# Splitting a half one step earlier, asking for an input first, and sending four outputs by another queue

## The chip, the cores and the metric

The kernel runs on one core of one Trainium2 chip. TensorE (PE in the rows) does the matmuls, VectorE (DVE) and ScalarE (ACT) the elementwise work, GpSimd (POOL) and SyncE (SP) mostly ask for transfers. Each engine takes its instructions strictly in the order in which they were written, so an instruction that waits holds up everything behind it on that engine. The metric is device time in microseconds (us). Smaller is better.

## The reference, cut to what matters

```python
def reference(...):
    x = attn(x)                          # a Fourier layer: (2, 3008, 256) -> 6016 tokens x 256
    h = x @ w_in                         # first layer, 2048 wide
    x = (h * clip(h + 3, 0, 6) / 6) @ w_out
    g = x @ w_gate                       # second layer, 1536 wide: the change lies here
    val = x @ w_val
    return (silu(g) * val) @ w_out2      # float32 throughout
```

## The kernel before

The kernel runs in three parts: the Fourier layer, the first layer, and the second layer (from 617 us on). The change lies in the second layer.

The 6016 tokens are cut into six pairs of halves (five pairs of 2 x 512 tokens, one of 2 x 448). A step works one pair against one block of 128 of the 1536 hidden columns, so a pair takes 12 steps and the layer has 72, counted q = 0 to 71. In a step the gate and value products of both halves are made by seven block products instead of eight (a scheme of sums and differences). Each float32 product is three matmuls on parts: a high part, which ScalarE casts, and a low part, the difference that VectorE takes (`low`, line 138). One product is three rows at lines 948, 949 and 950. In the order of the step on TensorE they are P (1), Tb (7), Q (2), P (6), Tb (4), P (5), and P (3), the last of which stands in the next step's code.

Each step follows one chain. `seed` copies P into Q (line 1316); ScalarE copies Tb (`c7`) and P (`cu`) into a ring `cc` before further products are added to those banks; `first_sum` adds `cu` to Tb (line 1321), silu follows (line 1322); `second_sum` adds `c7` to P (line 1327), silu follows (line 1308); the first half's result is h0 * Q (line 1254), the second half's h1 * P, once P (3) has been added. Both halves are then split into high and low (`parted`, lines 1292 and 138) and multiplied by the output weights into four accumulators (`share`, whose matmuls stand in `mm3`, lines 133 to 135; the third of them reads the low part).

Pair 0 (q = 0 to 11) and nearly all of the last pair (q = 61 to 71) run as `plain`, with four output products for each step: 33 matmuls in all. There the results of step q - 1 are split in the code of step q. The steps of pairs 1 to 4 run as `quad`; they take fewer output products, form sums of results of neighbouring steps (`units`, added on VectorE at line 1247 or by an adding transfer on POOL's queue at line 1250), and work on what remains in the next pair. The first quad, q = 12, still closes pair 0: it makes the last output products and sends four outputs of pair 0 (`outward`, `send_out`, line 1180).

Two side works run along. `operands` prepares the next pair's input: a load into `raw` (1 MB, one buffer, line 840), then eleven steps of one cast on ScalarE (line 806, in seven of them) and one subtraction on VectorE (lines 799 and 138). `todo.send()` does one of these at the end of each step. `out_sums` and `out_parts` prepare, in pair 0, the sums of the output weights for the middle pairs: in even steps four small subtractions on VectorE and one copy on ScalarE (lines 1222 to 1226), in odd steps two casts on ScalarE, two subtractions on VectorE and two transfers on POOL's queue (lines 1238 to 1243). Weights for a step come on SP's queue (`fetch`, line 868), asked for about three steps ahead into one of four slots.

Nothing schedules the work: the order on each engine is the order of the code.

Of the kernel before, what the change touches and what calls it, by code (L numbers as in the profile page):

```python
# [82 lines left out]
def fourier_moe_kernel(ctx: ExitStack, tc: tile.TileContext, x, lin, bias, w1, w2, fwd1, inv2, fwd2,  # L83
                       inv1, out):
    nc = tc.nc
# [179 lines left out]
    p = psf[0]([128, 512], "p0")  # L265
# [697 lines left out]
    todo = Todo()  # L963
# [136 lines left out]
    ring2 = {}  # L1100
# [73 lines left out]
        nc.tensor.matmul(o, wh, xh, start=False, stop=False, skip_group_check=True)  # L1174
        nc.tensor.matmul(o, wh, xl, start=False, stop=True, skip_group_check=True)

    def send_out(p, e, t, c, send=nc.sync):
        n = halves[p]
        at = pairs[p][0] + t * n
        send.dma_start(out[e * 128 : e * 128 + 128, at : at + n], c[:, :n])  # L1180
# [75 lines left out]
            nc.vector.scalar_tensor_tensor(out=o, in0=x, scalar=-1.0, in1=y, op0=ALU.mult, op1=ALU.mult)  # L1256

    def upper(before):
        p, k, odd, P, h, product, n = before
        product(P, 3)  # L1260
        times2(U(p, ("T3", "T2")[odd], k), h[:, :n], P[:, :n], 1 if odd else -1)

# [27 lines left out]
    def parted(x, n):  # L1290
        hi, lo = (take(c)[:, :n] for c in ("hi", "lo"))
        nc.scalar.copy(hi, x[:, :n])  # L1292
        low(lo, x[:, :n], hi)
        return hi, lo
# [20 lines left out]
    def seed(q, P, Q, n):  # L1315
        nc.scalar.copy(Q[:, :n], P[:, :n])  # L1316
        state.pop("silu", lambda: None)()
# [12 lines left out]
    def quad(q, before):  # L1330
        p, f = quads2[q]
        k, odd = divmod(f, 2)
        n = halves[p]
        old, i = p - 1, f
        waits, first = old > 0, q == NF
        a = (p, k - 1) if k else (p - 1, NK - 1)
        P, T = bank_p(F0 + q), one_bank(spot[0] + 3, [128, BLK], "Tb")
        if p == 1 and odd and f < NF - 1:
            Q = one_bank(spot[0], [128, BLK], "Q")
        else:  # L1340
            Q = bank_q([128, BLK], "Q")
        product = multiply(B[len(pairs) + p], F0 + q, n)
        product(P, 1, start=True)
        if waits:
            later(old, i, 0)
        else:
            product(T, 7, start=True)
        seed(q, P, Q, n)
        if first:
            x0 = parted(state["own"], n)  # L1350
            x1 = parted(upper_plain(before), n)
        else:
            upper(before)
        if waits:
            later(old, i, 1)
        if odd:
            x1 = halve(p, k, "T1")
            add_up(p, k, "T1", "T3")
            if a[0] > 0:
                add_up(*a, "T2", "T1")  # L1360
                add_apart(*a, "T4", "T2")
        elif a[0] > 0:
            x2, x3 = halve(*a, "T4"), halve(*a, "T2")
            add_up(*a, "T3", "T2")
        if waits and i % 3 == 2:
            phase(old, i // 3)
        if waits:
            product(T, 7, start=True)
        c7 = ring2["c"]()[:, :n]
        nc.scalar.copy(c7, T[:, :n])  # L1370
        if first:
            share(q, 0, 0, x0)
            outward(0, 0, 0)
        product(Q, 2)
        product(P, 6)
        if waits:
            ask(old + (i + 2) // NF, (i + 2) % NF)
        elif f == NF - 1:
            ask(1, 0)
            ask(1, 1)  # L1380
        if old + (i + 1) // NF > 0:
            part2(old + (i + 1) // NF, (i + 1) % NF)
        cu = ring2["c"]()[:, :n]
        nc.scalar.copy(cu, P[:, :n])
        if odd:
            live(p, 1, k, slot[F0 + q - 1][:, 14:16], x1)
            gone(q - 1)
            if f == NF - 1:
                then = begin(p)
        elif first:  # L1390
            share(q, 0, 1, x0)
            outward(0, 0, 1)
            share(q, 1, 0, x1)
        else:
            live(a[0], 2, a[1], slot[F0 + q - 1][:, 14:16], x2)
            if not k:
                corner(a[0])
        product(T, 4)
        h0 = first_sum(T, cu, n)
        if first:  # L1400
            outward(0, 1, 0)
            share(q, 1, 1, x1)
            gone(q - 1)
        elif not odd:
            live(a[0], 3, a[1], slot[F0 + q - 1][:, 16:18], x3)
            gone(q - 1)
            if not k:
                third(a[0])
        product(P, 5)
        h1 = second_sum(P, c7, n)  # L1410
        if first:
            outward(0, 1, 1)
            home.append(spots["double"])
        if q == len(quads2) - NF:
            own()
        times2(take("own")[:, :n] if p == len(pairs) - 1 else U(p, ("T1", "T4")[odd], k), h0, Q[:, :n],
               -1 if odd and p < len(pairs) - 1 else 1)
        state["own"] = spots["own"][-1]
        todo.send()
        silu(q, h1)  # L1420
        if f == NF - 1:
            then()
        return p, k, odd, P, h1, product, n

    def own():
        d = spots["double"] = home.pop()
        spots["own"] = [d[:, 0], d[:, 1]]

    def upper_plain(before):
        _, _, _, P, h, product, n = before  # L1430
        product(P, 3)
        s1 = take("own")
        times2(s1[:, :n], h[:, :n], P[:, :n], 1)
        return s1

    def plain(q, before):

        p, f = quads2[q] if q < len(quads2) else (None, None)
        pb = len(pairs) - 1 if q in LAST else 0
        old, i = pb - 1 if p else -1, f  # L1440
        n = halves[pb]
        early = old > 0 and f == 1
        if early:
            later(old, i, 0)
            later(old, i, 1)
        if before:
            s1 = upper_plain(before)
        if old > 0 and not early:
            later(old, i, 0)
            later(old, i, 1)  # L1450
        if before:
            x0 = parted(spots["own"][0], n)
        if p is None:
            x1 = parted(s1, n)
            for t, x in enumerate((x0, x1)):
                for e in range(2):
                    share(q, t, e, x)
                    if t and e:
                        a = acc.pop((t, e))
                        for o, c, copy, send in ((take("short"), slice(0, n // 2), nc.vector.tensor_copy, nc.sync),  # L1460
                                                 (take("h"), slice(n // 2, n), nc.scalar.copy, nc.scalar)):
                            copy(o[:, c], a[:, c])
                            at = pairs[pb][0] + n
                            send.dma_start(out[e * 128 : e * 128 + 128, at + c.start : at + c.stop], o[:, c])
                    else:
                        outward(pb, t, e)
            return None
        k, odd = divmod(f, 2)
        if early:
            add_up(old, NK - 1, "T2", "T1")  # L1470
            add_apart(old, NK - 1, "T4", "T2")
        T, Q = one_bank(spot[0] + 3, [128, BLK], "Tb"), bank_q([128, BLK], "Q")
        P = bank_p(F0 + (len(quads2) - NF if pb else q))
        product = multiply(B[len(pairs) + p], F0 + q, n)
        product(P, 1, start=True)
        if q == 0:
            fetch(F0 + 2)
            fetch(F0 + 3)
            nc.tensor.matmul(Q, slot[F0][:, 0], B[len(pairs)][1][:, 0], start=True, stop=True)
            end = end_of()  # L1480
            drain(2)
        seed(q, P, Q, n)
        if before:
            x1 = parted(s1, n)
        if old > 0 and i % 3 == 2:
            phase(old, i // 3)
        product(T, 7, start=True)
        c7 = ring2["c"]()[:, :n]
        nc.scalar.copy(c7, T[:, :n])
        if q == 0:  # L1490
            end()
            drain(2)
        else:
            share(q, 0, 0, x0)
        product(Q, 2)
        product(P, 6)
        if old > 0 and i + 1 < NF:
            part2(old, i + 1)
        if old > 0 and i + 2 < NF:
            ask(old, i + 2)  # L1500
        cu = ring2["c"]()[:, :n]
        nc.scalar.copy(cu, P[:, :n])
        if q == 0:
            drain(2)
        else:
            share(q, 0, 1, x0)
        product(T, 4)
        h0 = first_sum(T, cu, n)
        if q == 0:
            drain(len(pending))  # L1510
            lay_out_rest()
            own()
        product(P, 5)
        h1 = second_sum(P, c7, n)
        if q:
            share(q, 1, 0, x1)
            share(q, 1, 1, x1)
            gone(q - 1)
        times2(take("own")[:, :n], h0, Q[:, :n], 1)
        state["own"] = spots["own"][-1]  # L1520
        todo.send()
        silu(q, h1)
        if not p:
            (out_parts if odd else out_sums)(k)
        return p, k, odd, P, h1, product, n

    lay_out()
    ask_out(0)
# [69 lines left out]
```

## Time and profile before

| what | us |
|---|---|
| median of 3 runs | 1140.84 (1140.32 to 1141.79) |
| profiled execution | 1139.65 |
| its span in the trace | 1137.9 |
| TensorE busy | 1111.9 (98%) |
| VectorE busy | 963.4 (85%) |
| ScalarE busy | 803.8 (71%) |
| chain of waits: TensorE, VectorE, ScalarE, DMA | 78%, 12%, 4%, 3% |

Matmuls are pipelined: one that reads 512 columns shows 0.38 us, but the next starts 0.22 us after it. So the busy share of TensorE says little, and what is lost is read from the distance of two starts. An idle time that the trace gives in square brackets names the instruction that ended it.

### The profile page before, as it was taken

The page shows a single profiled execution, that of the slowest core. Times are in us where ns is not written, and L with a number is a line of the kernel's source. Part 1 is how long each engine was busy: PE and PEld are TensorE (multiplying, and loading weights), DVE is VectorE, ACT ScalarE, POOL GpSimd, SP SyncE. Part 2 cuts the span into 40 slices and gives each one's busy share as a digit, 9 for nine tenths or more (in the row PEclk, how much of TensorE's full clock was granted, in tenths as well). Part 3 has the DMA queues.
Part 4 walks back from the last instruction along what each step waited for, and adds up shares of the span by engine and source line. Part 5 has one row for each costly group of instructions (what it writes and reads, how often), then busy time and mean ns, then how long its engine had stood idle before and what let it go on. Part 6 is the DMA issues. An engine that isn't in the chain of part 4 may idle for free.

```text
span 1137.9 us, 19968 instructions
## 1 busy us (share of the span) xinstructions
PE 1111.9 (98%) x7397; PEld 973.0 (86%) x7397; DVE 963.4 (85%) x1703; ACT 803.8 (71%) x1491; POOL 72.7 (6%) x105
## 2 busy tenths in 40 slices
PE   8999999999999999999999999899999999999998
PEld 7989888888888888888999777687888888888997
DVE  6878887999999999999987676598999999998665
ACT  4767676788787887887777565567667777776555
POOL 3000016200000000000000000000000000000000
PEclk9999999999999999999999999899999999999999
DMA  7756335874474572753745554677877877878551
GB/s 286 292 183 226 121 109 190 269 234 167 148 241 152 167 254 99 234 214 106 257 145 185 217 199 176 217 231 232 259 231 227 261 248 231 263 240 249 195 199 74
DMA packets 82201, 234.18 MB, mean 206 GB/s; under 512 B 8180, under 2 KB 31892, under 8 KB 70648
## 3 DMA queue, kind: packets, MB, share of 16 engines
q1 hardware_dynamic: 75472, 216.20, 55.9%
q0 software_dynamic: 6336, 16.52, 5.4%
q8 instruction: 58, 0.95, 0.3%
q14 instruction: 39, 0.32, 0.1%
q10 hardware_dynamic: 296, 0.20, 0.1%
HBM read 180.98 MB, written 45.61 MB: 199 GB/s over the span
## 4 chain that ended last, share of the span: by engine, by line
PE 78%; DVE 12%; ACT 4%; DMA 3%; issue 2%; POOL 0%; DVEq 0%; ACTq 0%; SPq 0%; POOLq 0%
PE acc L135 8%; PE acc L133 8%; PE acc L134 8%; PE P L948 7%; PE P L950 6%; PE P L949 6%; PE Tb L948 3%; PE Tb L950 3%; PE Tb L949 3%; DMA raw<-Xd 2%; PE p L462 2%; PE p L368 2%; PE Q L948 2%; PE Q L949 2%; PE Q L950 2%
## 5 line engine op out<-in xcount | busy, mean ns | idle before, releaser
L618 ACT CAST gated<-r 128x512 fp32r<-128x512 f32 (+1 forms) x160 | 98.3, 614 | 64.4 <-DVE r L996 62.9
L138 DVE TENSOR_TENSOR gated<-r,gated 128x512 fp32r<-128x512 f32 (+1 forms) x160 | 107.9, 674 | 24.1 <-ACT gated L618 19.4
L133 PE MATMUL acc<-gated,w_o 128*128 128x512 f32 (+1 forms) x320 | 120.4, 376 | 0.0
L1322 ACT ACTIVATE hv<-hv 128x512 f32<-128x512 f32 (+1 forms) x72 | 44.8, 622 | 107.0 <-DVE hv L1321 107.0
L134 PE MATMUL acc<-gated,w_o 128*128 128x512 f32 (+1 forms) x320 | 119.6, 374 | 0.0
L135 PE MATMUL acc<-gated,w_o 128*128 128x512 f32 (+1 forms) x320 | 119.6, 374 | 0.0
L992 ACT ACTIVATE r<-hold,consts 128x512 f32<-128x512 f32 (+1 forms) x120 | 85.5, 712 | 14.2 <-DVE hold L1000 12.1
L948 PE MATMUL P<-xo,slot 128*128 128x512 f32 (+1 forms) x240 | 91.1, 380 | 2.4 <-DVE hold L1000 1.2
L950 PE MATMUL P<-xo,slot 128*128 128x512 f32 (+1 forms) x240 | 89.1, 371 | 0.0
L949 PE MATMUL P<-xo,slot 128*128 128x512 f32 (+1 forms) x240 | 89.1, 371 | 0.0
L996 DVE SCALAR_TENSOR_TENSOR r<-r,hold 128x512 f32<-128x512 f32 (+1 forms) x120 | 80.8, 674 | 2.5 <-ACT r L992 1.4
L1321 DVE TENSOR_TENSOR hv<-Tb,cc 128x512 f32<-128x512 f32 (+1 forms) x72 | 48.6, 675 | 33.9 <-PE Tb L950 33.9
L133 PEld LDWEIGHTS acc<-gated,w_o 128*128 128x128 f32 x320 | 60.5, 189 | 7.0
L135 PEld LDWEIGHTS acc<-gated,w_o 128*128 128x128 f32 x320 | 60.5, 189 | 6.9
L134 PEld LDWEIGHTS acc<-gated,w_o 128*128 128x128 f32 x320 | 60.5, 189 | 6.7
L133 PE MATMUL acc<-live,slot 128*128 128x512 f32 (+1 forms) x156 | 58.9, 378 | 0.8 <-ACT live L1292 0.8
L134 PE MATMUL acc<-live,slot 128*128 128x512 f32 (+1 forms) x156 | 58.4, 374 | 0.0
L948 PEld LDWEIGHTS P<-xo,slot 128*128 128x128 f32 x240 | 45.4, 189 | 13.5 <-DVE hold L1000 3.0
L1316 ACT COPY Q<-P 128x512 f32<-128x512 f32 (+1 forms) x72 | 40.8, 566 | 20.3 <-PE P L950 16.7
L1327 DVE TENSOR_TENSOR hv<-P,cc 128x512 f32<-128x512 f32 (+1 forms) x72 | 48.4, 672 | 6.1 <-PE P L950 6.1
L1153 ACT CAST parts<-units 128x1024 fp32r<-128x1024 f32 x48 | 50.5, 1052 | 0.0
L950 PEld LDWEIGHTS P<-xo,slot 128*128 128x128 f32 x240 | 45.5, 190 | 4.4
(251 smaller groups left out, 3332.9 us busy)
## 6 DMA issues: line engine op xcount, KB each, us to landing
slot<-Wd SPq DMA_DIRECT2D x48, 1024.0 KB
slot<-Sd SPq DMA_DIRECT2D x40, 896.0 KB
slot<-Wd SPq DMA_DIRECT2D x24, 1152.0 KB
st<-in_w SPq DMA_DIRECT2D x68, 256.0 KB
Wd<-slot SPq DMA_DIRECT2D x12, 1024.0 KB
chunk<-Vd SPq DMA_DIRECT2D x48, 256.0 KB
m<-in_fwd SPq DMA_DIRECT2D x12, 512.0 KB
Cd<-cs POOLq DMA_DIRECT2D x12, 512.0 KB, 5.1
```

Of the source, the lines that this page charges most:

```text
L133: nc.tensor.matmul(o, wl, xh, start=start, stop=False)
L134: nc.tensor.matmul(o, wh, xh, start=False, stop=False)
L135: nc.tensor.matmul(o, wh, xl, start=False, stop=stop)
L138: nc.vector.tensor_tensor(out=o, in0=full, in1=hi.bitcast(F32), op=ALU.subtract)
L618: nc.scalar.copy(hi[:, :n], g[:, :n])
L948: nc.tensor.matmul(o, wl, hi, start=start, stop=False, skip_group_check=not start)
L949: nc.tensor.matmul(o, wh, lo, start=False, stop=False, skip_group_check=not start)
L950: nc.tensor.matmul(o, wh, hi, start=False, stop=True, skip_group_check=not start)
L992: nc.scalar.activation(r[:, :n], x[:, :n], AF.Relu, bias=three)
L996: nc.vector.scalar_tensor_tensor(out=r[:, :n], in0=r[:, :n], scalar=6.0, in1=x[:, :n], op0=ALU.min, op1=ALU.mult)
L1153: nc.scalar.copy(hi, t[:, :, :n])
L1321: nc.vector.tensor_tensor(out=h, in0=T[:, :n], in1=cu, op=ALU.add)
```

## The change

It has five parts.

1. In pair 0 the first half's result is split at the end of its own step, in `plain`, and handed on with the other results; the next step only uses it.
2. In pair 0 `out_sums` and `out_parts` run in the next step's code, after the second half's split; the last of them falls into the first quad.
3. The first quad asks for the next pair's input (`todo.send()`) ahead of its other work, and not at its end.
4. The four outputs of pair 0 are asked for by POOL's queue, and not by SP's.
5. Two changes of order: in the steps of pair 1 ScalarE copies Tb (`c7`) right behind the seed and its silu, ahead of the splits; in the second step of the last pair the product Tb (7) comes ahead of P (1).

```diff
-    def send_out(p, e, t, c, send=nc.sync):
+    def send_out(p, e, t, c, send=None):
+        send = send or (nc.sync if p else nc.gpsimd)
...
     def quad(q, before):
...
+        c7 = ring2["c"]()[:, :n]
         seed(q, P, Q, n)
+        if not waits:
+            nc.scalar.copy(c7, T[:, :n])
         if first:
-            x0 = parted(state["own"], n)
+            todo.send()
+            x0 = before[-1]
             x1 = parted(upper_plain(before), n)
+            state.pop("side")()
         else:
             upper(before)
...
         if waits:
             product(T, 7, start=True)
-        c7 = ring2["c"]()[:, :n]
-        nc.scalar.copy(c7, T[:, :n])
+            nc.scalar.copy(c7, T[:, :n])
...
         state["own"] = spots["own"][-1]
-        todo.send()
+        if not first:
+            todo.send()
         silu(q, h1)
...
     def plain(q, before):
...
-        if before:
+        if before and before[-1]:
+            x0 = before[-1]
+        elif before:
             x0 = parted(spots["own"][0], n)
...
         product = multiply(B[len(pairs) + p], F0 + q, n)
+        if early:
+            product(T, 7, start=True)
         product(P, 1, start=True)
...
         if before:
             x1 = parted(s1, n)
+        state.pop("side", lambda: None)()
...
-        product(T, 7, start=True)
+        if not early:
+            product(T, 7, start=True)
...
         todo.send()
         silu(q, h1)
-        if not p:
-            (out_parts if odd else out_sums)(k)
-        return p, k, odd, P, h1, product, n
+        own_parts = None
+        if not pb:
+            own_parts = parted(state["own"], n)
+            state["side"] = lambda: (out_parts if odd else out_sums)(k)
+        return p, k, odd, P, h1, product, n, own_parts
```

On VectorE, from the first sum of one plain step with `out_sums` to that of the next, there stood before (`units<-hv,Q` is the first half's result, `units<-hv,P` the second half's, `live<-units,live` and `lows<-units,live` their low parts, `outs` the weight sums):

```order
L1321 TENSOR_TENSOR hv<-Tb,cc 128x512
L1327 TENSOR_TENSOR hv<-P,cc 128x512
L1254 TENSOR_TENSOR units<-hv,Q 128x512
L138 TENSOR_TENSOR xo<-T_7525,xo 128x512
L1224 SCALAR_TENSOR_TENSOR outs<-hv 128x128
L1224 SCALAR_TENSOR_TENSOR outs<-outs,hv 128x128
L1222 TENSOR_TENSOR outs<-hv 128x128
L1222 TENSOR_TENSOR outs<-hv,outs 128x128
L1254 TENSOR_TENSOR units<-hv,P 128x512
L138 TENSOR_TENSOR live<-units,live 128x512
L138 TENSOR_TENSOR lows<-units,live 128x512
L1321 TENSOR_TENSOR hv<-Tb,cc 128x512
```

and at the same place there stands now:

```order
L1322 TENSOR_TENSOR hv<-Tb,cc 128x512
L1328 TENSOR_TENSOR hv<-P,cc 128x512
L1255 TENSOR_TENSOR units<-hv,Q 128x512
L138 TENSOR_TENSOR xo<-T_7525,xo 128x512
L138 TENSOR_TENSOR live<-units,live 128x512
L1255 TENSOR_TENSOR units<-hv,P 128x512
L138 TENSOR_TENSOR lows<-units,live 128x512
L1225 SCALAR_TENSOR_TENSOR outs<-hv 128x128
L1225 SCALAR_TENSOR_TENSOR outs<-outs,hv 128x128
L1223 TENSOR_TENSOR outs<-hv 128x128
L1223 TENSOR_TENSOR outs<-hv,outs 128x128
L1322 TENSOR_TENSOR hv<-Tb,cc 128x512
```

The first half's low part has moved ahead of five instructions, the second half's ahead of the four small ones; those now stand right before the next first sum.

On SP's queue, where pair 0 ends, the difference of the two orders is (`slot` is a step's weights, `raw` the next pair's input, `out_t` the outputs):

```order
 L868 DMA slot<-Wd_64 128x2304
 L868 DMA slot<-Wd_65 128x2048
-L1180 DMA out_t<-sums 128x512
-L1180 DMA out_t<-hv 128x512 x2
+L840 DMA raw_7897<-Xd 128x2x1024
 L868 DMA slot<-Wd_66 128x2304
-L1180 DMA out_t<-sums 128x512
-L840 DMA raw_7949<-Xd 128x2x1024
 L868 DMA slot<-Wd_67 128x2048
```

The input is asked for one weight fetch and four outputs earlier, and the outputs have left this queue.

## Rows read from the trace of the kernel before

**Rows 1.** page, TensorE's granted clock in 40 slices, tenths of full speed:

```profile
PEclk9999999999999999999999999899999999999999
```

**Rows 2.** timeline of TensorE, plain step q = 11 (start us, us, engine, line, operation):

```profile
703.69 0.38 PE L948 MATMUL P<-gs,slot 128*128 128x512 f32 x1
...
705.85 0.38 PE L134 MATMUL acc<-live,slot 128*128 128x512 f32 x1
706.88 0.48 PE L135 MATMUL acc<-lows,slot 128*128 128x512 f32 x1 [0.66 <-DVE lows L138]
707.20 0.38 PE L948 MATMUL Q<-xy,slot 128*128 128x512 f32 x1
```

**Rows 3.** timeline of TensorE, first Q matmul of steps 1 and 12:

```profile
626.33 0.38 PE L948 MATMUL Q<-xy,slot 128*128 128x512 f32 x1
...
715.30 0.38 PE L948 MATMUL Q<-xo,slot 128*128 128x512 f32 x1
```

**Rows 4.** timeline of ACT, the same plain step:

```profile
703.34 0.63 ACT L1308 ACTIVATE hv<-hv 128x512 f32<-128x512 f32 x1
...
704.18 0.62 ACT L1292 CAST live<-units 128x512 fp32r<-128x512 f32 x1
```

**Rows 5.** timeline of DVE, the same plain step, up to the next first sum:

```profile
703.40 0.69 DVE L1254 TENSOR_TENSOR units<-hv,Q 128x512 f32<-128x512 f32 x1
...
704.61 0.28 DVE L1224 SCALAR_TENSOR_TENSOR outs<-hv 128x128 f32<-128x128 f32 x1
...
705.55 0.68 DVE L1254 TENSOR_TENSOR units<-hv,P 128x512 f32<-128x512 f32 x1
706.14 0.68 DVE L138 TENSOR_TENSOR lows<-units,live 128x512 fp32r<-128x512 f32 x1
...
710.06 0.69 DVE L1321 TENSOR_TENSOR hv<-Tb,cc 128x512 f32<-128x512 f32 x1 [2.46 <-PE Tb L950]
```

**Rows 6.** timeline of SP's queue, q = 11 and first quad:

```profile
711.28 0.32 SPq L868 DMA_DIRECT2D slot<-Wd  x1
...
721.54 0.45 SPq L1180 DMA_DIRECT2D out_t<-sums  x1
```

**Rows 7.** chain of waits, 720 to 732 us (start us, us, what):

```profile
722.04 8.60 DMA raw<-Xd
```

**Rows 8.** timeline of DVE and ACT around the input's old and new reader:

```profile
712.05 0.68 DVE L138 TENSOR_TENSOR xo<-raw,xo 128x512 fp32r<-128x512 f32 x1
...
725.86 0.63 ACT L1322 ACTIVATE hv<-hv 128x512 f32<-128x512 f32 x1 [1.59 <-DVE hv L1321]
```

**Rows 9.** timeline of TensorE, from the second quad to the third:

```profile
727.24 0.38 PE L950 MATMUL P<-xo,slot 128*128 128x512 f32 x1
731.81 0.80 PE L948 MATMUL Q<-xo,slot 128*128 128x512 f32 x1 [4.19 <-ACT Q L1316]
...
737.00 0.38 PE L133 MATMUL acc<-live,slot 128*128 128x512 f32 x1
```

**Rows 10.** timeline of all engines in quad q = 16, and Q of q = 23:

```profile
745.50 0.48 PE L948 MATMUL Q<-xo,slot 128*128 128x512 f32 x1
...
745.91 0.60 ACT L1266 CAST live<-units 128x512 fp32r<-128x512 f32 x1
...
747.29 0.57 ACT L1370 COPY cc<-Tb 128x512 f32<-128x512 f32 x1
747.38 0.48 PE L135 MATMUL acc<-live,slot 128*128 128x512 f32 x1
...
747.92 0.48 PE L948 MATMUL Tb<-xo,slot 128*128 128x512 f32 x1
...
786.47 0.48 PE L948 MATMUL Q<-xo,slot 128*128 128x512 f32 x1
```

**Rows 11.** timeline of TensorE, last pair, second step:

```profile
1047.02 0.35 PE L950 MATMUL P<-xo,slot 128*128 128x448 f32 x1
1048.21 0.46 PE L948 MATMUL P<-xo,slot 128*128 128x448 f32 x1 [0.84 <-DVE units L1254]
```

More of the change, by code (lines that the diff above doesn't have):

```diff
@@ L1258, in upper @@
     def upper(before):
-        p, k, odd, P, h, product, n = before
+        p, k, odd, P, h, product, n, *_ = before
         product(P, 3)
@@ L1422, in quad @@
             then()
-        return p, k, odd, P, h1, product, n
+        return p, k, odd, P, h1, product, n, None
     def own():
@@ L1429, in upper_plain @@
     def upper_plain(before):
-        _, _, _, P, h, product, n = before
+        _, _, _, P, h, product, n, *_ = before
         product(P, 3)
@@ L1522, in plain @@
         silu(q, h1)
-        if not p:
-            (out_parts if odd else out_sums)(k)
-        return p, k, odd, P, h1, product, n
+        own_parts = None
[3 more added lines that the diff above has]
+        return p, k, odd, P, h1, product, n, own_parts
     lay_out()
```

## The prediction

> **What bounds the kernel now.** I read the granted clock by slices first. It is full everywhere but for one slice, about 740 us into the span [rows 1], so the question is where TensorE waits, and for whom. Next I read TensorE's timeline stage by stage and looked for two starts that stand further apart than usual. In the second layer the usual distance is 0.216 us: from 703.69 to 705.85 there are ten [rows 2]. TensorE works nearly without a break in the middle pairs. It loses time in three places that the change touches: once in every plain step of pair 0, once in one long wait where pair 1 begins, and once in the last pair.
>
> The plain step: the third matmul of the first output product reads the low part of the first half. It could have started at 705.85 + 0.216 = 706.07 and started at 706.88; the next came 0.32 after it and not 0.216 [rows 2]. That is 0.81 + 0.10 = 0.91 us. Over all steps: from the first Q matmul of step 1 to that of step 12 it takes 715.30 - 626.33 = 88.97 us [rows 3]. Eleven times 33 matmuls of 0.216 are 78.4, so 10.6 us are lost, nearly one for each step.
>
> The long wait: TensorE's next start was due at 727.24 + 0.22 = 727.46 and came at 731.81. From there to 737.00 it ran twelve matmuls in 5.19 us, 0.43 each, the level of 1.2 GHz; at 2.4 GHz, with 0.216 each, they take 2.59 [rows 9]. So the wait itself costs 4.35 and the clock 2.60 behind it, together 6.95 us. The chain of waits names the cause: the load of the next pair's input, 8.60 us from 722.04 on [rows 7]. A cast on ScalarE stands in that queue for it, ahead of the seed that TensorE needs.
>
> **The plain steps, parts 1 and 2 of the change.** Before, ScalarE casts the first half at 704.18, behind the silu of 703.34 and a small copy [rows 4]. VectorE's own product ends at 703.40 + 0.69 = 704.09, but the low part stands behind four small subtractions (704.61 to 705.55) and the second half's product, and starts at 706.14 [rows 5]. So VectorE's order made it late, and the cast did not. Now the cast can start when the product is there and the silu through, at 704.1, and ends at 704.74 (0.62 long); the input's subtraction on VectorE is out of the way at 704.61 [rows 5]. The low part takes 0.68 and is there at 705.45, 0.6 ahead of 706.07. In the steps that cast a part of the next input (seven of twelve), a cast of 0.6 may stand ahead on ScalarE; I let it cost up to 0.51, since the next instruction starts before it ends: 705.96, still 0.1 ahead. So the wait goes.
>
> What is late next? The small subtractions now stand before the next first sum. VectorE waits there 2.46 us for TensorE [rows 5]. A step that is 0.95 shorter leaves 1.5 of them; the work of VectorE in a step is the same as before, and only its new waits inside (for two casts) come out of these 1.5. In the odd steps ScalarE has two casts of weight parts ahead of the copy of Tb, for which the product Tb (4) waits. Between Tb (7) and Tb (4) TensorE has twelve matmuls, 12 x 0.216 = 2.6 us; ScalarE has the seed, the split's cast, those two and the copy, five at a pace of about 0.5 [rows 4], 2.5. That just fits. I keep 0.3 for such remainders in all. Gain 10.3; the ends are 10.6 (all of it) and 0 (an equal wait takes its place). I take the upper region, since both queues were worked through and have room.
>
> **The input, part 3, and the outputs, part 4.** Before, SP asks for the input after four outputs, the last at 721.54 [rows 6], which waits for the last accumulator's copy. Now nothing of that stands ahead. The one buffer must be free: its last reader is VectorE's subtraction at 712.05, through at 712.73 [rows 8]. The weight fetch ahead of the load on the queue was sent at 711.28 [rows 6]. So the load goes out at 712.75, 9.3 us earlier than 722.04. With 8.60 us it lands at 721.35. The cast that needs it stands behind the silu of 725.86 [rows 8], at 726.4; the first quad has the wait of a plain step too, so all after it comes 0.9 sooner: 725.5. The load is 4.1 us early. Then the wait goes, and with it the idle time ahead of the slow clock. The third quad will have the small loss of its kind that it now hides under the long wait, as q = 16 shows (0.42, next part but one); I take off 0.45. Gain 6.5, with ends 6.95 and 0.
>
> The four outputs go to POOL's queue. Nothing reads them, and POOL has no compute here; the next user of that queue is an adding transfer three quads later. They cost nothing as long as they don't hold the load back. The Trainium skill speaks against a part of this: the page DMA: Bandwidth & Descriptors, section Issuing engines are not separate DMA queues, says that transfers asked for by different engines run on the same 16 DMA engines and interleave, so that another queue only saves time at the asker. No run here shows outputs and input on two queues. By it the outputs still share the engines with the load, and only the earlier request helps. The sum stands on the earlier request alone, and the rival "the load is late" is what that rule could bring.
>
> **The copy of Tb in pair 1, part 5.** In q = 16 the split's cast starts at 745.91, the copy of Tb at 747.29, ending at 747.86, and the product Tb (4) starts at 747.92 in place of 747.38 + 0.216 = 747.60, with 0.10 more behind it [rows 10]. With the copy first that wait goes, but the split's cast and so its low part come 0.5 later: the cast starts at 746.4, ends at 747.0, the low part (0.69) at 747.7, and the third matmul of the output product, at 747.38 now, starts at 747.75; Tb (4) at 748.07. That is 0.15 worse. In quads without an input cast ahead I find about 0.1 better, and in the odd quads, where nothing is lost today, up to 0.1 worse. Bounds: from q = 16 to q = 23 it takes 786.47 - 745.50 = 40.97 [rows 10], and four quads of 27 and three of 24 matmuls are 180 x 0.216 = 38.9, so at best 2.1 are won; at worst each of 11 quads pays the full 0.5, 5.5 lost. The nearest row is the step worked through: I take 0.4 lost.
>
> **The last pair, part 5.** P (1) starts at 1048.21 in place of 1047.02 + 0.19 = 1047.21, since its bank waits for VectorE [rows 11]. Three matmuls of Tb (7), 0.19 each, now fill 0.57 of that. Q (2) then comes that much sooner behind P (1) and waits a little for the seed. I take 0.4, with ends 0 and 0.6.
>
> **The sum.** 1139.65 (the profiled execution: span 1137.9 and 1.75 around it) - 10.3 - 6.5 + 0.4 - 0.4 = 1122.85. The median of the runs lies 1.19 above that execution, so I predict 1124.0 us, 16.8 less than 1140.84.
>
> **The rivals.**
> - Half of the plain wait stays. Seven of twelve steps have the input's cast on ScalarE, and there I have only 0.1 to spare; if half a microsecond remains in each: 1124.0 + 3.5 = 1127.5. For it speaks how little is spare; against it that the cast before wasn't what was late [rows 4, 5].
> - The load is late all the same, because weights, weight sums and outputs share the transfer engines with it. It needs more than 8.6 + 4.1 = 12.7 us for that. Against it: the 8.60 were measured with an output sent half a microsecond before it [rows 6, 7]. If the whole wait stays: 1124.0 + 6.5 = 1130.5.
> - The late splits of pair 1 cost the full 5.5: 1124.0 + 5.1 = 1129.1. VectorE is dense there, and a low part that is late pushes all behind it.
> - Slower than before: VectorE becomes the bound of the plain steps. A step takes 88.97 / 11 = 8.09 us and VectorE's work in it 8.09 - 2.46 = 5.6 [rows 3, 5]. The new order lets it wait for a cast twice in a row. Up to 1.5 us of such waits cost nothing. Above that each step pays, twelve times; 16.8 / 12 = 1.4 more, 2.9 us in all, eats the whole gain. At 3.1 us: 1140.84 + 12 x 0.2 = 1143. Against it: two casts of 0.62 don't make 2.9.
> - The change does not do what it says: the load is asked for early but held on the queue, and the plain wait only moves to the next matmul. Then both gains are gone and the time is about 1141.
>
> **How the numbers follow.** The forecast as summed has 0.65. Half of the plain wait 0.14, the late load 0.08, the late splits 0.08, slower 0.02, no change 0.03. The likeliest one's own range, by 10.6 and 9 in the plain steps and by the bounds of the copy of Tb, is 1121.5 to 1126. The range that holds 8 in 10 takes in the next cases: 1121 to 1130. About 0.2% is what a measurement of this kernel can tell from no change, 2.3 us; faster by more 0.95, same 0.03, slower 0.02.
>
> **What would show it.** Right: in the plain steps the distance of two Q matmuls falls from 8.1 to 7.1 or 7.2, and no row of the third output matmul names a low part; `raw` is sent within 1 us of the last subtraction on its old content and no cast waits for it; the slice of slow clock is gone. In pair 1 the pace stays within 0.1 of today's. Wrong: a wait of half a microsecond in the steps with an input cast, a wait for `raw`, or VectorE without idle time before the first sum.

## The result and the profile after

The changed kernel takes 1123.26 us (median of 4 runs, 1122.92 to 1125.64) against 1140.58 (4 runs, 1140.17 to 1141.79): a ratio of 0.9851 with a 95% interval of 0.9834 to 0.9868, or 15.1 to 18.9 us less. The forecast was 1124.0, with 1121 to 1130 as its range. The profiled execution took 1123.0.

The page of the kernel after: the span, TensorE's granted clock in 40 slices, and the chain's shares by engine.

```profile
span 1121.2 us, 19961 instructions
...
PEclk9999999999999999999999999999999999999999
...
PE 85%; DVE 8%; ACT 3%; DMA 2%; issue 1%; POOL 0%; ACTq 0%; DVEq 0%; SPq 0%; POOLq 0%
```

The slice of slow clock [rows 1] is gone. VectorE's share of the chain fell from 12% to 8%, TensorE's rose from 78% to 85%.

**Where the time went.** The first Q matmul of each step marks the second layer into stretches. This table is worked out from those rows, in each kernel's own profiled execution:

| us | Q of step 0 at | steps 0–12 | 12–15 | 15–24 | 24–60 | 60–71 | 0–71 |
|---|---|---|---|---|---|---|---|
| before | 618.05 | 97.25 | 24.94 | 53.80 | 247.53 | 84.26 | 507.78 |
| after | 616.31 | 86.55 | 19.11 | 54.88 | 248.22 | 84.23 | 492.99 |
| difference | −1.74 | −10.70 | −5.83 | +1.08 | +0.69 | −0.03 | −14.79 |

The span is 16.7 shorter, of which 14.8 lie in the second layer and 1.74 ahead of it, where both kernels run the same instructions; the rest, 0.2, is behind step 71. So the total hit better than its parts did, which is luck: see below.

**The plain steps.** The timeline of TensorE in the kernel after, plain step 10, and the Q matmuls of steps 1 and 12:

```profile
624.24 0.38 PE L948 MATMUL Q<-xy,slot 128*128 128x512 f32 x1
...
695.30 0.38 PE L134 MATMUL acc<-live,slot 128*128 128x512 f32 x1
695.52 0.38 PE L135 MATMUL acc<-lows,slot 128*128 128x512 f32 x1
695.73 0.38 PE L948 MATMUL Q<-xy,slot 128*128 128x512 f32 x1
...
702.86 0.38 PE L948 MATMUL Q<-xo,slot 128*128 128x512 f32 x1
```

The third output matmul, which waited 0.66 for `lows` [rows 2], now starts 0.22 after the second, and the Q matmul 0.21 after that. From step 1 to step 12 it is 702.86 − 624.24 = 78.62 us in place of 88.97 [rows 3]: 0.2 above the 78.4 that eleven times 33 matmuls take. Eight of the eleven distances are 7.12 or 7.13, the floor; three are 7.21 or 7.22.

The timeline of ScalarE and VectorE in the same stretch of the kernel after:

```profile
692.86 0.69 DVE L1255 TENSOR_TENSOR units<-hv,Q 128x512 f32<-128x512 f32 x1
...
693.64 0.62 ACT L1293 CAST live<-units 128x512 fp32r<-128x512 f32 x1 [0.21 <-DVE units L1255]
...
694.29 0.69 DVE L138 TENSOR_TENSOR lows<-units,live 128x512 fp32r<-128x512 f32 x1
...
696.32 0.69 DVE L138 TENSOR_TENSOR hv<-units,live 128x512 fp32r<-128x512 f32 x1 [0.74 <-ACT live L1293]
...
696.93 0.28 DVE L1225 SCALAR_TENSOR_TENSOR outs<-hv 128x128 f32<-128x128 f32 x1
...
698.60 0.69 DVE L1322 TENSOR_TENSOR hv<-Tb,cc 128x512 f32<-128x512 f32 x1 [0.65 <-PE Tb L950]
```

The first half's low part starts 1.43 behind its product (694.29 − 692.86), where it was 2.74 before (706.14 − 703.40 [rows 5]). It is through 0.54 ahead of the matmul that reads it. The second half's low part waits 0.74 for its cast, the small subtractions stand behind it, and VectorE still idles 0.65 for TensorE ahead of the next first sum, where it was 2.46 [rows 5]. TensorE sets the pace.

**The input.** SP's and POOL's queues with VectorE's and ScalarE's rows on `raw`, kernel after:

```profile
699.81 0.32 SPq L868 DMA_DIRECT2D slot<-Wd  x1
700.59 0.68 DVE L138 TENSOR_TENSOR xo<-raw,xo 128x512 fp32r<-128x512 f32 x1
701.34 0.53 SPq L840 DMA_DIRECT2D raw<-Xd  x1
...
706.63 0.59 POOL L1181 DMA_DIRECT2D out_t<-sums  x1
...
709.17 0.54 POOL L1181 DMA_DIRECT2D out_t<-sums  x1
...
714.36 0.60 ACT L806 CAST xy<-raw 128x512 fp32r<-128x512 f32 x1
```

The load goes out 0.07 after the buffer's last reader is through (700.59 + 0.68 = 701.27), ahead of all four outputs, 1.5 us ahead of step 12's first Q matmul (702.86); before, it went out 6.74 behind it (722.04 [rows 7] against 715.30 [rows 3]). The cast no longer waits, and the 4.35 us wait and the half clock [rows 9] are gone.

**The copy of Tb.** All engines in quad q = 16 of the kernel after, the quad of [rows 10]:

```profile
727.41 0.48 PE L948 MATMUL Q<-xo,slot 128*128 128x512 f32 x1
727.82 0.56 ACT L1352 COPY cc<-Tb 128x512 f32<-128x512 f32 x1
728.29 1.14 ACT L1267 CAST live<-units 128x512 fp32r<-128x512 f32 x2
728.93 0.69 DVE L138 TENSOR_TENSOR live<-units,live 128x512 fp32r<-128x512 f32 x1 [0.30 <-ACT live L1267]
728.96 0.48 PE L133 MATMUL acc<-live,slot 128*128 128x512 f32 x1
729.68 0.48 PE L135 MATMUL acc<-live,slot 128*128 128x512 f32 x1
730.00 0.38 PE L948 MATMUL Tb<-xo,slot 128*128 128x512 f32 x1
```

Counted from the Q matmul, the copy comes at 0.41 in place of 1.79, the split's first cast at 0.88 in place of 0.41. The third output matmul starts at 2.27 in place of 1.88, and Tb (4) at 2.59 in place of 2.42. The 0.48 on the matmuls at L133 and L135 marks two stops: the first output matmul reads the high part, and that is late now too.

In most odd quads only the third output matmul is late. TensorE in q = 17, kernel after:

```profile
733.89 0.38 PE L948 MATMUL Q<-xo,slot 128*128 128x512 f32 x1
...
735.68 0.48 PE L135 MATMUL acc<-hv,slot 128*128 128x512 f32 x1
```

It starts 1.79 behind Q; with the copy put back (see below) it starts at 1.73 and shows 0.38, no stop.

**The last pair.** TensorE and VectorE in its second and third steps, kernel after:

```profile
1031.73 0.46 PE L948 MATMUL P<-xo,slot 128*128 128x448 f32 x1 [0.28 <-DVE units L1255]
...
1033.17 0.46 PE L948 MATMUL Q<-xo,slot 128*128 128x448 f32 x1
...
1035.01 1.22 DVE L138 TENSOR_TENSOR parts<-units,parts 128x1024 fp32r<-128x1024 f32 x1 [0.76 <-ACT parts L1153]
1036.15 0.62 DVE L1322 TENSOR_TENSOR hv<-Tb,cc 128x448 f32<-128x448 f32 x1
...
1041.02 0.35 PE L948 MATMUL Q<-xo,slot 128*128 128x448 f32 x1
```

P (1) waits 0.28 in place of 0.84 [rows 11], and Q of step 61 comes 0.35 sooner behind Q of step 60 (8.10 in place of 8.45). But the next Q comes 7.85 behind it in place of 7.54. VectorE's next first sum stands behind a low part of 1.22 us that itself waits 0.76 for ScalarE, and so does not start sooner.

### The profile page after: what moved, and what is told of

Read it like the earlier page. It is cut to its first block, busy times and chain, and to the rows that moved or that the text cites. A ratio compares the mean times of both kernels' runs of the same rounds, so it can differ in the third digit from the quotient of the medians.

```text
span 1121.2 us, 19961 instructions
## 1 busy us (share of the span) xinstructions
PE 1107.2 (99%) x7397; PEld 970.4 (87%) x7397; DVE 965.5 (86%) x1703; ACT 803.1 (72%) x1491; POOL 74.6 (7%) x109
## 4 chain that ended last, share of the span: by engine, by line
PE 85%; DVE 8%; ACT 3%; DMA 2%; issue 1%; POOL 0%; ACTq 0%; DVEq 0%; SPq 0%; POOLq 0%
PE acc L133 9%; PE acc L135 9%; PE acc L134 8%; PE P L948 8%; PE P L950 7%; PE P L949 7%; PE Tb L948 4%; PE Tb L950 4%; PE Tb L949 4%; PE Q L948 2%; DMA raw<-Xd 2%; PE p L462 2%; PE p L368 2%; PE Q L949 2%; PE Q L950 2%; PE D L1174 2%
## 5 line engine op out<-in xcount | busy, mean ns | idle before, releaser
L133 PE MATMUL acc<-gated,w_o 128*128 128x512 f32 (+1 forms) x320 | 120.4, 376 | 0.0
L135 PE MATMUL acc<-gated,w_o 128*128 128x512 f32 (+1 forms) x320 | 119.6, 374 | 0.0
L133 PEld LDWEIGHTS acc<-gated,w_o 128*128 128x128 f32 x320 | 60.5, 189 | 7.0
L135 PEld LDWEIGHTS acc<-gated,w_o 128*128 128x128 f32 x320 | 60.5, 189 | 6.9
L133 PE MATMUL acc<-live,slot 128*128 128x512 f32 (+1 forms) x156 | 58.8, 377 | 0.4 <-ACT live L1293 0.4
```

Of the source, the lines that this page charges most:

```text
L133: nc.tensor.matmul(o, wl, xh, start=start, stop=False)
L135: nc.tensor.matmul(o, wh, xl, start=False, stop=stop)
```

## The experiments

Nine kernels ran. "0–71" is the time from the first Q matmul of step 0 to that of step 71, in each one's own profiled execution; the rest is as in the table above.

| us | median (runs) | ratio to before, 95% | Q of step 0 at | 0–12 | 12–15 | 15–24 | 24–60 | 0–71 |
|---|---|---|---|---|---|---|---|---|
| part 1 alone | 1130.07 (4) | 0.9925 [0.9904, 0.9947] | 615.70 | 88.49 | 25.06 | 53.80 | 248.54 | 500.16 |
| part 2 alone | 1131.09 (4) | 0.9933 [0.9913, 0.9953] | 618.12 | 87.26 | 27.88 | 53.82 | 248.89 | 502.12 |
| part 3 alone | 1133.69 (4) | 0.9952 [0.9934, 0.9970] | 616.51 | 97.27 | 18.65 | 53.82 | 248.43 | 502.44 |
| part 4 alone | 1139.36 (10) | 0.9997 [0.9987, 1.0006] | 616.85 | 97.27 | 24.60 | 53.80 | 248.68 | 508.62 |
| after, copy of Tb put back | 1122.67 (4) | 0.9856 [0.9839, 0.9874] | 617.78 | 86.55 | 18.64 | 53.82 | 248.38 | 491.62 |
| the same, all inputs early | 1119.45 (5) | 0.9822 [0.9806, 0.9839] | 617.63 | 86.57 | 18.65 | 53.81 | 245.92 | 489.16 |
| after, small sums twice | 1128.63 (1) | – | 620.60 | 87.86 | 19.11 | 54.86 | 248.30 | 494.36 |
| after, small sums four times | 1138.73 (1) | – | 619.65 | 98.84 | 19.12 | 54.86 | 248.32 | 505.36 |
| after, outputs and Tb (7) put back | 1125.17 (4) | 0.9873 [0.9857, 0.9890] | 618.49 | 86.55 | 19.11 | 54.85 | 248.77 | 493.55 |

**Part 1 alone**, the split at its own step's end; all else as before:

```diff
+            own_parts = parted(state["own"], n)
-            x0 = parted(state["own"], n)
+            x0 = before[-1]
```

> The kernel before with part 1 alone: the first half is split at the end of its own step, the weight sums stay right behind it. Theory: the first half's low part was late only because four small subtractions and the second half's product stood ahead of it on VectorE, so moving the split alone frees it. Then the stretch from the Q matmul of step 0 to that of step 12 falls from 97.25 us to about 87 and the time to about 1130. Rival: the sums are what fills VectorE, and as long as they stand ahead of the second half's split the wait only moves to the second half; then the stretch stays above 92 us and the time above 1135.

Steps 0–12 fell by 8.76. Steps 3, 5, 7 and 9 now take 7.43 or 7.44 and the others from step 1 on 7.18 to 7.31, over the floor of 7.12. The rows of ScalarE and TensorE in one of them, part 1 alone:

```profile
639.69 0.58 ACT L1492 COPY cc<-Tb 128x512 f32<-128x512 f32 x1
639.90 0.38 PE L135 MATMUL acc<-live,slot 128*128 128x512 f32 x1
640.32 0.48 PE L948 MATMUL Tb<-gs,slot 128*128 128x512 f32 x1
```

Tb (4) was due at 639.90 + 0.22 = 640.12, but its copy ends at 640.27. The split's cast on ScalarE, ahead of that copy, waits for the second half's product, and that product still stands behind the four small subtractions. So part 1 alone frees the third output matmul but leaves a smaller stop behind the same cause.

**Part 2 alone**, the sums of the output weights behind the second split:

```diff
-            (out_parts if odd else out_sums)(k)
+            state["side"] = lambda: (out_parts if odd else out_sums)(k)
...
+        state.pop("side", lambda: None)()
```

> The kernel before with part 2 alone: the weight sums run behind the second half's split of the next step, the first half is split there as before. Theory: without the four small subtractions ahead of it, the low part stands behind the input's subtraction and the second half's product only, and is done about 0.1 us ahead of its need; the stretch from step 0 to step 12 falls from 97.25 to 87 to 89 us. Rival: the second half's product waits for TensorE, and the low part behind it stays late; then the stretch stays above 92 us.

VectorE's and TensorE's rows of a plain step, part 2 alone:

```profile
696.22 0.69 DVE L138 TENSOR_TENSOR lows<-units,live 128x512 fp32r<-128x512 f32 x1
...
697.07 0.38 PE L135 MATMUL acc<-lows,slot 128*128 128x512 f32 x1
697.28 0.38 PE L948 MATMUL Q<-xy,slot 128*128 128x512 f32 x1
```

Steps 1 to 10 take 7.12 or 7.13 each, the floor, without the early split: the low part still stands behind the second half's product, but no longer behind the work on the weight sums, and that is enough. So this work made the wait of these steps: the four small subtractions in every second step, and the two subtractions of `out_parts` in those between, which the prediction does not name as a cause. Only step 11, into the first quad, keeps 8.10 in place of 7.12. TensorE there, in the kernel before and in part 2 alone:

```profile
714.25 0.48 PE L133 MATMUL acc<-live,slot 128*128 128x512 f32 x1 [0.42 <-ACT live L1292]
```

```profile
704.34 0.48 PE L133 MATMUL acc<-live,slot 128*128 128x512 f32 x1 [0.41 <-ACT live L1293]
```

In this one step the split's cast was late, not the low part alone, and the early split cures that. Beside part 2 the early split is worth the 0.98 of that one step, 0.71 net of the tenths that the kernel after loses in others. The two gains don't add: 8.76 and 9.99 alone, 10.70 together.

The stretch 12–15 grew by 2.94. The load of the input took longer than before, though SP's queue around it was the same: a weight fetch 0.87 ahead of it and one 2.38 behind, 0.88 and 2.37 before. The chain of waits in part 2 alone:

```profile
712.12 11.02 DMA raw<-Xd
```

**Part 3 alone**, the input asked for first, with the outputs still on SP:

```diff
         if first:
+            todo.send()
...
-        todo.send()
+        if not first:
+            todo.send()
```

> The kernel before with part 3 alone: the first quad asks for the next input first, the four outputs stay on SP's queue. Theory: the moment of the request decides, so the load lands before it is needed, the slow clock is gone, and from the Q matmul of step 12 to that of step 15 it takes 18.4 to 19.1 us in place of 24.94; the time falls by about 6.3 to 1134.3. Rival: the outputs on the same queue hold the load or its neighbours back, and more than half of the wait stays: above 22 us.

SP's and ScalarE's rows, part 3 alone:

```profile
711.28 0.53 SPq L840 DMA_DIRECT2D raw<-Xd  x1
...
724.88 0.60 ACT L806 CAST xy<-raw 128x512 fp32r<-128x512 f32 x1
```

No cast waits for `raw`; the stretch 12–15 takes 18.65 in place of 24.94, and nothing else moved. This is the whole of the input's gain, 6.29, without POOL's queue.

**Part 4 alone**, the outputs by POOL's queue, the input where it was:

```diff
+        send = send or (nc.sync if p else nc.gpsimd)
```

> The kernel before with part 4 alone: the four outputs go by POOL's queue, the input is asked for at the step's end as before. Theory: the request still stands behind the weight fetch of 721.16, goes out about 0.5 us sooner and lands at most 1 us sooner; from step 12 to step 15 it takes 23.9 to 24.9 us and the time stays within 1 us of before. Rival: the four outputs ahead of it on the queue were what delayed the load; then the stretch falls below 22 us.

The chain of waits in part 4 alone, and ScalarE's cast behind it:

```profile
718.61 10.10 DMA raw<-Xd
```

```profile
728.74 0.62 ACT L806 CAST xy<-raw 128x512 fp32r<-128x512 f32 x1 [3.42 <-DMA raw<-Xd]
```

With the outputs out of SP's way the load is asked for 4.49 behind step 12's Q matmul and not 6.74, but takes 10.10 us and not 8.60. The request is 2.25 sooner, where the expectation had 0.5: the weight fetch ahead of it had been held by the outputs too. The cast's wait shrinks from 4.16 to 3.42, the stretch by 0.34, and the time is the same, 0.9997. The Trainium skill's rule that the prediction weighed (DMA: Bandwidth & Descriptors, Issuing engines are not separate DMA queues) is that transfers asked for by different engines run on the same DMA engines and interleave. This run agrees with it: two of the outputs were asked for while the load ran, and of the 2.25 saved at the asker 1.50 were lost again in the transfer.

**The copy of Tb put back** behind the splits in the kernel after:

```diff
-        if not waits:
-            nc.scalar.copy(c7, T[:, :n])
...
-            nc.scalar.copy(c7, T[:, :n])
+        nc.scalar.copy(c7, T[:, :n])
```

> The changed kernel with one part undone: in pair 1 the copy of Tb stands behind the splits again. Theory: the copy ahead of the splits makes them late and is a net loss, so from the Q matmul of step 12 to that of 15 it takes 18.65 us in place of 19.11 and from 15 to 24 53.8 in place of 54.88; the time is about 1.5 below that of the changed kernel. Rival: the slower pace of pair 1 comes from the outputs on POOL's queue or from the transfers packed closer; then 15 to 24 stays above 54.6.

TensorE in the same quad, q = 16, with the copy put back:

```profile
728.23 0.48 PE L948 MATMUL Q<-xo,slot 128*128 128x512 f32 x1
...
730.12 0.48 PE L135 MATMUL acc<-live,slot 128*128 128x512 f32 x1
...
730.66 0.48 PE L948 MATMUL Tb<-xo,slot 128*128 128x512 f32 x1
```

From Q the third output matmul starts at 1.89 and Tb (4) at 2.43, as before the change. The stretches 12–15 and 15–24 are 0.47 and 1.06 shorter than in the kernel after: the copy first costs 1.53. By quads, from TensorE's starts: 0.17 in each of q = 15, 17, 19 and 21, which lost at most 0.08 with the copy behind; 0.40 in each of q = 13 and 23; 0.06 to 0.08 in the three with a cast of the input (q = 14, 16, 22); 0.08 or 0.09 won back in q = 18 and in q = 20. The medians don't show the expected 1.5: they are 0.6 us apart, and the ratios to before, 0.9856 and 0.9851, have overlapping intervals. The same stretches in all other runs show it: 15–24 takes 53.80 to 53.82 with the copy behind and 54.85 to 54.88 with the copy first, and 12–15, where no cast waits for the input, 18.64 or 18.65 and 19.11 or 19.12.

**The same, with all inputs asked for first**, in the first quads of pairs 2, 3 and 4 too:

```diff
-        if first:
+        if f == 0:
             todo.send()
...
-        if not first:
+        if f:
             todo.send()
```

> As the kernel before this one, and the first quads of pairs 2, 3 and 4 also ask for their next input first. In the changed kernel a cast waits 0.71 to 0.84 us for that input in each of them, and the seed behind it. Theory: the three waits go and 24 to 60 falls from 248.2 by 1.2 to 1.8 us; the time is about 3 us below that of the changed kernel. Rival: the input then shares the transfer engines with a weight fetch and the weight parts that are due sooner, and one of those becomes late; then 24 to 60 does not fall or grows.

In the kernel after, the load of pair 2 goes out behind an output, and its first cast waits. SP's and ScalarE's rows, kernel after:

```profile
781.65 0.53 SPq L840 DMA_DIRECT2D raw<-Xd  x1
...
789.22 0.62 ACT L806 CAST xo<-raw 128x512 fp32r<-128x512 f32 x1 [0.75 <-DMA raw<-Xd]
```

The same rows with all inputs asked for first:

```profile
776.02 0.53 SPq L840 DMA_DIRECT2D raw<-Xd  x1
...
788.19 0.60 ACT L806 CAST xo<-raw 128x512 fp32r<-128x512 f32 x1
```

No cast waits any more. Steps 24–60 take 245.92 in place of 248.38, 2.46 less, which is what the three casts had waited with the copy put back (1.03 + 0.70 + 0.77 = 2.50), and more than the 1.2 to 1.8 expected. The median of 1119.45 is the lowest of all, 1.8% below before (1139.2 on that chip); its highest run, 1120.5, is below the lowest of the kernel with only the copy put back, 1122.19. It is the fastest version that ran; against the kernel after, its ratio to before is 0.9822 and not 0.9851, with intervals that overlap at their ends.

**The small sums twice and four times** in the kernel after; the repeats write the same values:

```diff
+        for _ in range(2):   # 4 in the second kernel
         minus(g[:, 0], A[:, 1], A[:, 3], -1)
         ...
```

> The changed kernel with the four small subtractions of the weight sums done twice in each of the six even steps of pair 0, about 0.95 us more of VectorE's work right before a first sum, the outputs the same. VectorE idles 0.73 to 0.78 us there in the changed kernel. Theory (the first sum decides the pace from that point on): 0.2 to 0.4 us late six times, step 0 to step 12 grows from 86.55 to 87.8 to 89 us. Rival (there is more slack behind the first sum): it stays below 87.2.

> The same with the four subtractions done four times, about 2.9 us more in each of six steps. Theory: all above the idle 0.75 us is paid, 2.1 us six times, step 0 to step 12 grows from 86.55 to about 99 us. Rival: half a microsecond or more is absorbed further on, in the slack of the splits, and it ends below 96.

The slower rival said that VectorE would set the pace of the plain steps. Four subtractions take 0.93 (629.65 to 630.58 in the run with two sets). The next first sum with the sums twice; and with them four times, the matmul that then waits for VectorE too:

```profile
631.51 0.69 DVE L1323 TENSOR_TENSOR hv<-Tb,cc 128x512 f32<-128x512 f32 x1
```

```profile
632.43 0.68 DVE L1323 TENSOR_TENSOR hv<-Tb,cc 128x512 f32<-128x512 f32 x1
633.76 0.48 PE L948 MATMUL P<-gs,slot 128*128 128x512 f32 x1 [1.48 <-DVE hv L1329]
```

With them twice VectorE has no idle left in the six steps that bear them, and the stretch costs 1.31 more, 0.22 for each of the six. Four times, 2.79 added, costs 12.29, 2.05 each. So about 0.7 us (0.93 − 0.22, or 2.79 − 2.05) were free in each. VectorE's idle there is 0.53 to 0.73 in the kernel after; the 0.75 to 0.78 in the expectation is that of the steps between. Above what is free nearly each microsecond on VectorE is one of the kernel: the second kernel adds 1.86 to a step of the first and takes 1.83 longer. The rival's mechanism is real, and the change stays 0.7 us on the good side of it.

**The outputs on SP again and Tb (7) behind P (1) again** in the kernel after:

```diff
-        send = send or (nc.sync if p else nc.gpsimd)
+        send = send or nc.sync
...
-        if early:
-            product(T, 7, start=True)
```

> The changed kernel with two parts undone that lie in different stages: the four outputs of pair 0 go by SP's queue again (read from step 12 to 15), and in the last pair Tb (7) stands behind P (1) again (read from step 60 to 71). Theory: the queue doesn't matter once the input is asked for first, 12 to 15 stays at 19.1 us within 0.2; the last pair loses the 0.04 us that it won, 84.27 in place of 84.23. Rival: with the early request the outputs on SP's queue hold up the weight fetch behind them or the input, and 12 to 15 grows by half a microsecond or more.

Every stretch up to step 24 is within 0.03 of the kernel after, and steps 60–71 take 84.27 and not 84.23. Neither part is worth anything that can be seen. The median is 1.9 higher than that of the kernel after; in the profiled execution 2.2 of the span's 2.9 lie ahead of step 0 and 0.55 in steps 24–60, the two stretches that vary without these parts (see the last section).

## Why the prediction was right, and where its sizes were off

The verdict, the time and the mechanisms of the two large terms held. Term by term, against the profiled execution of before:

- **Plain steps: 10.3 predicted, 10.35 measured** from step 1 to step 12, and 0.35 in step 0, which the sum had left out. The reason was the right one for ten of the eleven: part 2 alone shows that the work on the weight sums made the low part late, and not the cast. In the step into the first quad, which the prediction took for the same wait, it was the cast (0.42). What the prediction did not see is that either part frees most of the wait alone, and the two overlap almost wholly. Of its 0.3 of remainders 0.2 came. The rival "half of the plain wait stays" is refuted by the 7.12 to 7.22 of the steps.
- **What is late next:** the prediction left VectorE 1.5 us of idle less its waits for two casts; measured are 0.53 to 0.78, since VectorE waits 0.74 for one of the two. With the repeated sums the margin was measured at about 0.7. VectorE is nearer to setting the pace than the 2.9 us of the rival's break-even suggest: the first stop comes from 0.7 on.
- **The input: 6.5 predicted, 6.29 measured** with the old order of the copy (part 3 alone; 6.30 with the copy put back), 5.83 in the kernel after, since 0.47 of the next term falls in the same stretch. The load was asked for within 0.07 us of the buffer's release and no cast waited, so the rival of a late load is refuted. The queue of the outputs had no part in it, as the sum had it.
- **The copy of Tb: 0.4 lost predicted, 1.53 measured.** This term was mis-sized, within its bounds (2.1 won to 5.5 lost). The step worked through was right, 2.57 predicted for Tb (4) behind Q and 2.59 measured, and the even quads nearly cancel (−0.09 to +0.08). The fault lies in the odd quads, for which the prediction had "up to 0.1 worse". In q = 15 to 21 they lose 0.17 each, since the later low part now stops the third output matmul. In q = 13 and 23 they lose 0.40 each: there, as in q = 16, the first output matmul stops too, since the high part that it reads is late. The sign that the prediction named, a pace of pair 1 within 0.1 of before, came only in the even quads.
- **The last pair: 0.4 won predicted, 0.04 measured.** The 0.35 of step 61 came, and 0.31 went in step 62, where VectorE's order behind the adding of `parts` sets the next stop. The prediction followed the freed time only to Q (2).
- **What hid the sizes:** the execution after began its second layer 1.74 sooner, without an edit ahead of it, and spent 0.69 more in steps 24–60. Of these 0.49 are longer waits of casts for loads (see the last section), and 0.18 lie in step 59. That step takes 6.72 or 6.73 in each kernel with part 1 and 6.55 in each without, so part 1 costs something there that the prediction did not have; why stays open. The second layer alone gained 14.79; by the terms it would have been 16.8. The total fits to 0.1 in the profiles (16.7 against 16.8) only because 1.74 from ahead of the change covers most of what the terms fell short. That closeness is luck; the two large terms are not.

## What to carry to other kernels

When a matmul waits for a value, look at what stands ahead of its producer on the same engine, before the producer's own inputs: here small subtractions that nobody was waiting for, in every second step four of 0.28 us, cost nearly 1 us in each step, and moving them, or the producer, freed most of it. The load's wait was cured by asking earlier, at the moment its buffer was free; another queue gained nothing. And a change of order in a repeated step is priced for every kind of step, also for those that lose nothing today: here q = 17 and 19 went from no loss to 0.17 each.

## What was not expected of the hardware

**One transfer, 8.6 to 11.0 us.** The load of the same 1 MB took 8.60, 8.69, 10.10 and 11.02 us in the four runs in which a cast waited for it (before, and parts 1, 4 and 2 alone). The engines' busy time in that stretch (TensorE, its weight loads, VectorE, ScalarE, POOL; granted clock, DMA share, GB/s) for before, part 4 alone and part 2 alone:

```profile
722.04:730.64 8.60, 5.58 (x24) 4.37 (x24) 3.96 (x6) 2.70 (x5) 0.00 (x0) 0.97 1.02 370
```

```profile
718.61:728.71 10.10, 7.74 (x34) 5.91 (x33) 5.84 (x9) 4.17 (x8) 1.08 (x2) 1.00 0.99 349
```

```profile
712.12:723.14 11.02, 5.59 (x24) 4.37 (x24) 3.96 (x6) 2.70 (x5) 0.00 (x0) 0.87 0.92 314
```

The DMA share is 0.92 to 1.02 over each stretch; how much of it was the load's own is not shown. Why part 2 alone got only 314 GB/s, with the same requests on SP's queue around it, stays open. POOL's two transfers of weight sums went out 4.2 us ahead of the load there, 6.8 in part 1 alone and 8.4 before, and in the microsecond ahead of the load the share was 1.00 in part 2 alone and 0.54 in the other two. Whether that is the reason was not tried.

**Two stretches vary without an edit.** The second layer began between 615.70 and 620.60 us over the eleven profiled executions, though the instructions ahead of it are the same, and steps 24–60 took 247.53 to 248.89 in the ten of them in which three casts wait for a load. Most of the second is told by these waits: their sum is 1.81 before, 2.30 after and 3.05 in part 2 alone. Without them and without step 59, 239.2 to 239.3 are left in all eleven. Why the first varies stays open. A median of four runs doesn't wholly average that out, which is why parts of 1 us are read from stretches here and not from medians.
